# Block 0's triangular steps without GpSimd beside them, block 1's steps moved beside block 0's dense units, and stores queued behind the next loads

## The chip, the cores and the metric

One core of a Trainium2 chip runs the whole program. Its engines are TensorE (PE in the profile; its weight loads are PEld), VectorE (DVE), ScalarE (ACT), GpSimd (POOL) and SyncE (SP), whose queue issues the DMAs. The metric is device time in microseconds (us), the median of repeated runs. Beside these stands one profiled execution, from which every duration below comes.

## The reference, cut to what matters

Three stages follow one another: a delta-rule attention over 4 batches, 8 heads, 768 steps of width 48; a gated feed-forward layer on the 3072 tokens (384 to 2048 to 384); and a dense mixture of 8 experts (384 to 1024 to 384) weighted by a balanced gate.

```python
k_n = k / (np.linalg.norm(k, axis=-1, keepdims=True) + 1e-06)
...
    y[:, :, t] = np.einsum('bhd,bhde->bhe', q[:, :, t], state)
    v_old = np.einsum('bhde,bhd->bhe', state, kt)
    state = state + bt[:, :, :, None] * np.einsum('bhd,bhe->bhde', kt, vt - v_old)
...
h = x @ w_in
sp = np.where(h > 20.0, h, np.log1p(np.exp(np.minimum(h, 20.0))))
g = h * np.tanh(sp)
return (g @ w_out).astype(np.float32)
...
    h = np.maximum(x @ w1[e], 0.0)
    ye = h @ w2[e]
    out += P[:, e:e + 1] * ye
```

## The kernel before

**Blocks and units.** The sequence is cut into 6 blocks of 128 steps for each batch and head. The recurrence of a block becomes a unit triangular system, solved in closed form, and only the state (48 by 48 per batch and head) passes from block to block. After a block's attention, its 512 tokens go through dense units: 16 units of the feed-forward layer (`s0` to `s15`) and 8 units of expert 0 (`s16` to `s23`); `MARKS` counts these places, with four more, `f1` to `f4`, between the two layers. Experts 1 to 7 follow after all blocks. In one dense unit TensorE runs nine matmuls of 512 columns into `psh` (L299) and nine more (L840), each product in three passes of a high and a low part: `xh`, `xl`, `gh` and `gl` are such parts.

**Attention of a block.** Scores of the keys (`st_g`, L590 and L591) land in `gx`; `mb` (`prep_mb`, L539) is the mask with the norms, put on block 0's scores as they leave PSUM (L570) and on block 1's afterwards by GpSimd (`mask_g`, L612). `lane_in_ops` brings the 32 by 32 diagonal blocks into the tile `lane` by transposes, one of all partitions (L622) and two of 32 partitions (L623), and `elim_ops` inverts them in 60 dependent steps on `lane`, a product (L635) and a sum (L641) in turn. `st_lane_out` transposes back (L650, L651). Then TensorE works through `st_m1` (L677), `st_m2` (L691) and the chain of stages z, w, s, y for both pairs (L711, L729, L747, L763) up to `x1` (L770), from which ScalarE makes `xh` (L773) and VectorE `xl` (L458, a helper's line that many VectorE operations share).

**Weights.** The 16 weights of the feed-forward layer arrive as 64-bit numbers. For each, ScalarE scales one half (L205), VectorE decodes in three operations (L188, L191, L196; called a trio below), ScalarE rounds to the high part (L251) and GpSimd subtracts for the low part (L252) into one of six slots `w`. SP stores each converted weight to DRAM (`wd`, L256), and from block 1 on loads it back (L245). Expert weights arrive plain and skip the decoding.

**The prologue.** Block 0's attention runs before any dense unit. `run_warm` puts extra matmuls on the tile `spare` (L874) between its stages. GpSimd meanwhile masks block 0's queries (`mask_p`, L560), scales its values (`prep_v`, L546), and makes and masks block 1's scores. Block 1's 60 steps are dealt out by hand: `elim1` hands most to GpSimd, in the prologue and in the first dense units, and the rest to VectorE, and `drain_elim` or its like closes them at `MARKS[m0]`.

**Order.** Each engine runs its own list in order, waiting on semaphores. Inside the dense units, `fill` and `rate` let queued steps (`eq`) in between by their written costs, and `PLACES` says at which mark each stage of the next blocks stands: for block 0, `m0` is 5 and the steps of block 2 begin at mark 24.

```python
        def elim1(n, eng):
            elim_eng[0] = eng
            for _ in range(min(n, len(ops1))):
                ops1.popleft()()
```

## Time and profile before

| what | us |
|---|---|
| median of 3 runs (2372.46 to 2373.16) | 2372.52 |
| the profiled execution's own time | 2370.98 |
| its span | 2369.2 |
| PE busy | 2298.2 (97%) |
| DVE, ACT, POOL busy | 801.2, 559.9, 471.2 |
| mean granted TensorE clock | 0.971 |

The span is what the instructions cover; the execution's own time lies 1.8 us above it. Busy shares are means over the whole run: TensorE's gaps all lie in the first fifth, where the attention of the blocks is interleaved, so the argument reads that stretch by itself. A record's duration includes time in which an operation stood blocked after it had begun.

### The profile page before, as it was taken

What the parts mean: (1) busy time and instruction counts of PE and PEld (TensorE: products, weight loads), DVE (VectorE), ACT (ScalarE), POOL (GpSimd) and SP (SyncE); (2) the same over time, 40 slices, a digit from 0 to 9 for tenths busy, and PEclk for the clock granted to TensorE, in tenths of its full rate; (3) what the DMA queues carried; (4) which work ended last, traced back from release to release, by engine and by line L of the source; (5) the groups of instructions that cost most, each with busy time, mean ns of one, the idle gap of its engine ahead of it and who ended that gap; (6) DMA issues with size and microseconds to landing.
All of it is one profiled execution on the core that took longest, in us unless ns stands there. A gap on an engine that the chain in (4) does not pass through costs nothing.

```text
span 2369.2 us, 36112 instructions
## 1 busy us (share of the span) xinstructions
PE 2298.2 (97%) x15492; PEld 1992.1 (84%) x15492; DVE 801.2 (34%) x1369; ACT 559.9 (24%) x999; POOL 471.2 (20%) x370
## 2 busy tenths in 40 slices
PE   8688899999999999999999999999999999999998
PEld 4477778878788888899999999999999999999998
DVE  8884725527162104431222222222222122212222
ACT  5244332332323232211211211121121111112111
POOL 5686442341412121310200100020020011001000
PEclk6799999999999999999999999999999999999999
DMA  5357643637344454410100100010010001000111
GB/s 173 134 195 211 211 154 129 211 114 238 131 164 148 162 198 140 167 40 1 54 1 1 37 17 1 1 54 1 1 54 1 1 20 34 1 1 27 27 27 27
DMA packets 79727, 196.00 MB, mean 83 GB/s; under 512 B 7696, under 2 KB 50448, under 8 KB 79568
## 3 DMA queue, kind: packets, MB, share of 16 engines
q1 hardware_dynamic: 79568, 193.70, 24.8%
q8 instruction: 122, 2.00, 0.3%
q14 instruction: 37, 0.30, 0.0%
HBM read 161.43 MB, written 32.24 MB: 82 GB/s over the span
## 4 chain that ended last, share of the span: by engine, by line
PE 90%; DVE 6%; DMA 2%; POOL 1%; issue 1%; ACT 0%; SPq 0%; DVEq 0%; POOLq 0%; ACTq 0%
PE psh L299 42%; PE o L321 30%; PE x L840 8%; PE y L321 3%; DVE t L635 1%; DVE lane L641 1%; PE psa L590 1%; PE psa L729 1%; PE psa L763 1%; DVE lane L623 1%; PE psa L711 1%; PE psa L860 1%; PE psa L747 1%; PE psa L677 1%; DMA wd<-w 0%
## 5 line engine op out<-in xcount | busy, mean ns | idle before, releaser
L299 PE MATMUL psh<-xh,w 128*128 128x512 f32 x2052 | 662.7, 404 | 13.7 <-DMA w<-wd 6.7
L314 DVE SCALAR_TENSOR_TENSOR hl<-psh,hh 128x512 fp32r<-128x512 f32 x384 | 265.1, 690 | 1111.8 <-ACT hh L313 1111.7
L313 ACT ACTIVATE hh<-psh 128x512 fp32r<-128x512 f32 x384 | 229.7, 598 | 1312.1 <-PE o L321 1154.5
L299 PEld LDWEIGHTS psh<-xh,w 128*128 128x128 f32 x2052 | 381.1, 191 | 91.2 <-issue 12.2
L299 PE MATMUL psh<-xl,w 128*128 128x512 f32 x1026 | 412.0, 402 | 4.2 <-DVE xl L458 4.2
L321 PE MATMUL o<-w,hh 128*128 128x384 f32 x1584 | 405.5, 337 | 0.0
L321 PEld LDWEIGHTS o<-w,hh 128*128 128x128 f32 x1584 | 288.2, 188 | 19.8 <-issue 4.9
L321 PE MATMUL o<-wx,hh 128*128 128x384 f32 x1104 | 282.0, 336 | 0.0
L321 PE MATMUL o<-w,hl 128*128 128x384 f32 x792 | 267.0, 337 | 0.0
L299 PE MATMUL psh<-xh,wx 128*128 128x512 f32 x828 | 258.3, 393 | 0.0
L299 PEld LDWEIGHTS psh<-xl,w 128*128 128x128 f32 x1026 | 196.3, 191 | 51.2 <-DVE xl L458 5.9
L321 PEld LDWEIGHTS o<-wx,hh 128*128 128x128 f32 x1104 | 201.5, 188 | 13.1 <-issue 2.1
L829 POOL TENSOR_TENSOR gl<-x,gh 128x512 fp32r<-128x512 f32 x96 | 127.5, 1328 | 420.0 <-ACT gh L828 416.2
L252 POOL TENSOR_TENSOR w<-raw,w 128x768 fp32r<-128x768 f32 x41 | 75.7, 1848 | 669.9 <-ACT w L251 669.8
L321 PE MATMUL o<-wx,hl 128*128 128x384 f32 x552 | 186.0, 337 | 0.0
L299 PEld LDWEIGHTS psh<-xh,wx 128*128 128x128 f32 x828 | 153.5, 188 | 25.2
L299 PE MATMUL psh<-xl,wx 128*128 128x512 f32 x414 | 163.4, 395 | 0.0
L840 PE MATMUL x<-gh,w 128*128 128x512 f32 x576 | 150.7, 397 | 0.0
L321 PEld LDWEIGHTS o<-w,hl 128*128 128x128 f32 x792 | 148.6, 188 | 0.0
L840 PEld LDWEIGHTS x<-gh,w 128*128 128x128 f32 x576 | 107.5, 189 | 24.9
L252 POOL TENSOR_TENSOR wx<-raw,wx 128x768 fp32r<-128x768 f32 x23 | 42.4, 1845 | 399.7 <-ACT wx L251 399.7
L321 PEld LDWEIGHTS o<-wx,hl 128*128 128x128 f32 x552 | 103.6, 188 | 0.0
(165 smaller groups left out, 2358.2 us busy)
## 6 DMA issues: line engine op xcount, KB each, us to landing
w<-wd SPq DMA_DIRECT2D x120, 768.0 KB, 4.4
raw<-in_w_dram SPq DMA_DIRECT2D x128, 192.0 KB, 2.6
wd<-w SPq DMA_DIRECT2D x24, 768.0 KB, 4.3
kq<-in_qkb_dram SPq DMA_DIRECT2D x20, 256.0 KB, 6.9
vt<-in_vtok_dram SPq DMA_DIRECT2D x6, 768.0 KB, 8.6
kq<-in_w_in_dram SPq DMA_DIRECT2D x12, 384.0 KB, 4.7
kq<-in_w_out_dram SPq DMA_DIRECT2D x12, 384.0 KB, 5.6
y0d<-xr SPq DMA_DIRECT2D x6, 768.0 KB, 4.7
```

The source lines that it names most:

```text
L252: nc.gpsimd.tensor_tensor(out=w[:, 1], in0=r, in1=w[:, 0].bitcast(F32), op=ALU.subtract)
L299: mm(ps, lhsT=wi(u, pw, kc), rhs=(xh, xl)[px][:, kc, :], start=(n == 0), stop=(n == 3 * KD - 1))
L313: nc.scalar.activation(out=h, in_=ps, func=AF.Relu)
L314: nc.vector.scalar_tensor_tensor(out=l, in0=ps, scalar=0.0, in1=h.bitcast(F32), op0=ALU.max, op1=ALU.subtract)
L321: mm(o[t], lhsT=(h, l)[ph][:, t * 128:(t + 1) * 128], rhs=wo(u, pw, 0, DM), start=(f == 0 and n == 0), stop=(f == U2 - 1 and n == 2))
L590: mm(ps[0:64, :, i], lhsT=k[64:64 + D, 0, h, :], rhs=k[64:64 + D, 0:2, h, :], start=True, stop=True)
L623: + [(1.14, lambda p=p: nc.vector.transpose(out=lane[p:p + 32], in_=v[p:p + 32, 32:64, :])) for p in (32, 96)]
L635: eng[0].tensor_tensor(out=slot[0], in0=lane[:, s + 1:32, s:s + 1].to_broadcast([128, n, s]), in1=lane[:, s:s + 1, 0:s].to_broadcast([128, ...
L641: eng[0].tensor_tensor(out=lane[:, s + 1:32, 0:s], in0=lane[:, s + 1:32, 0:s], in1=slot[0], op=ALU.add)
L677: mm(ps[p + 32:p + 64, i], lhsT=g[p:p + 32, t, h, 32:64], rhs=t11[p:p + 32, b, :], start=True, stop=True)
L829: nc.gpsimd.tensor_tensor(out=l, in0=p, in1=h.bitcast(F32), op=ALU.subtract)
L840: mm(x2ps[c][k], lhsT=wo(u, pw, k * 128, k * 128 + 128), rhs=(h, l)[pg], start=(f == 0 and n == 0), stop=(f == U1 - 1 and n == 2))
```

## The change

Seven edits, with the names used below.

1. Block 0's steps get VectorE to themselves: `mask_p(0)`, block 1's `mb` and `mask_g(1)` leave the stretch of the steps, and `prep_v(0)` goes from GpSimd to ScalarE (`prep_v_act`). Block 1's squares (`prep_ss(1)`) and norms come later, the norms by a GpSimd power (`prep_pow`) instead of ScalarE's root and VectorE's `root_ops`.
2. One transpose into `lane` instead of three (`lane_in_one`), after ScalarE has copied the diagonal blocks of two partition groups into place (`diag_left`); GpSimd clears the copies afterwards (`diag_clear`). `lane_in_ops` stays for blocks 2 to 5.
3. All 60 steps of block 1 go to VectorE, through the queue `eq`, beside block 0's dense units, closed at mark 9 (`m0` 9 instead of 5); the chain of block 1 and the scores of block 2 move to later marks, block 2's steps to mark 26 (24 before). `rate` is 0.6 in block 0 (0.4 before).
4. The prologue decodes and converts 4 weights (6 decoded, 5 converted before).
5. A weight's store goes to SP after the next raw loads (`late_stores`).
6. The stores of `y0` and `x2` go later in their block (`late_xr`).
7. `load_vt(0)` stands before `load_kq(1)`.

```diff
+    late_stores = deque()
+
+    def flush_stores():
+
+        while late_stores:
+            late_stores.popleft()()
...
-        if ch in w_dram:
-            nc.sync.dma_start(out=w_dram[ch], in_=w.bitcast(F32))
         n = order_of[i] + 2
         if n < len(firsts):
             if kind(firsts[n]) == "plain":
                 fetch(firsts[n])
+        flush_stores()
+        if ch in w_dram:
+            late_stores.append(lambda: nc.sync.dma_start(out=w_dram[ch], in_=w.bitcast(F32)))
...
+        def diag_left(c, t):
+
+            g = gx(c)[:, t]
+            for p in (32, 96):
+                nc.scalar.activation(out=g[p:p + 32, :, 0:32], in_=g[p:p + 32, :, 32:64], func=AF.Copy)
+
+        def diag_clear(c):
+            for p in (32, 96):
+                nc.gpsimd.memset(gx(c)[p:p + 32, :, :, 0:32].rearrange("p t h x -> p (t h) x"), 0.0)
+
+        def lane_in_one(c):
+            v = gx(c).rearrange("p t h x -> p x (t h)")
+            return [
+                (1.94, lambda: nc.vector.transpose(out=lane, in_=v[:, 0:32, :])),
+                (0.09, lambda: nc.vector.memset(lane.rearrange("p t i -> p (t i)")[:, 0:1024:33], 1.0)),
+                (0.0, lambda: diag_clear(c)),
+            ]
...
-            nc.sync.dma_start(out=y0_dram[c], in_=y)
+            late_xr.append(lambda: nc.sync.dma_start(out=y0_dram[c], in_=y))
...
-            for _, op in lane_in_ops(0):
+                diag_left(0, t)
+            for _, op in lane_in_one(0):
                 op()
...
-            for t in range(4):
-                prep_ss(1, t)
-            prep_root(1)
...
-            el(12)
-            for op in root_ops(1) + norm_ops(1, ALL):
-                el(1)
-                op()
             for t in range(4):
-                prep_mb(1, t, nc.gpsimd)
+                prep_ss(1, t)
             for t in range(2):
-                mask_p(0, t)
-            for t in range(2):
-                prep_v(0, t)
                 first_r(0, t)
-            for t in range(4):
-                mask_g(1, t, nc.gpsimd)
-            for t in range(2, 4):
-                prep_v(0, t)
-                mask_p(0, t)
-            for n in range(3):
+            for n in range(2):
                 begin_decode(n)
-            el(len(e0) - 16)
+            el(len(e0) - 24)
...
-            in1 = deque(op for _, op in lane_in_ops(1))
-            in1.popleft()()
-            elim_eng = [nc.gpsimd]
-            ops1 = deque(op for _, op in elim_ops(1, elim_eng))
...
+            prep_pow(1, ALL)
+            for op in norm_ops(1, ALL):
+                op()
+            for t in range(2):
+                mask_p(0, t)
+            for t in range(2):
+                prep_mb(1, t, nc.gpsimd)
...
-            step(4, 6, 5, 6)
             converts(4)
+            for t in range(2, 4):
+                prep_mb(1, t, nc.gpsimd)
+            for t in range(4):
+                mask_g(1, t, nc.gpsimd)
+                diag_left(1, t)
+            eq.extend(lane_in_one(1) + elim_ops(1))
...
-            (5, spread(5 + 3, 26, 2, 16), 21 - 5,
-             [21 - 2, 21 - 1, 21, 21 + 1], spread(21, 27, 2, 8), 18, 26, 24),
+            (9, [12, 12, 13, 13, 14, 14, 15, 15, 17, 18, 19, 19, 20, 20, 21, 21], 16,
+             [19, 20, 22, 23], [22, 22, 23, 23, 24, 24, 25, 26], 18, 26, 26),
...
-                rest[MARKS[m0]].append(drain_elim if c else lambda: elim1(60, nc.vector))
+                rest[MARKS[m0]].append(drain_elim)
...
-                rate(0.4 if c == 0 else 0.6)
+                rate(0.6)
...
-                    if not c and f < m0:
-                        elim1(10, nc.gpsimd)
```

The built programs differ most at four places. On VectorE at the end of the prologue, before, the three operations for `xl` stand behind a group of block 1's steps:

```order
L635 TENSOR_TENSOR t_160<-lane 128x220 [waits Pool_49]
L641 TENSOR_TENSOR lane<-lane,t_160 128x11x20 [waits DVE_49]
L635 TENSOR_TENSOR t_160<-lane 128x210 [waits DVE_49]
L641 TENSOR_TENSOR lane<-lane,t_160 128x10x21 [waits DVE_49]
L635 TENSOR_TENSOR t_160<-lane 128x198 [waits DVE_49]
L641 TENSOR_TENSOR lane<-lane,t_160 128x9x22 [waits DVE_49]
L458 TENSOR_TENSOR xl_1199<-psa,xh_1198 128x512 [waits Activation_49] x3
L458 TENSOR_TENSOR us_155<-psa,us_156 48x384 [waits PE_49]
```

Now, on VectorE at the same place (line numbers are those of the changed file: L655 is the transpose into `lane`, L467 the helper), the last trio of the prologue and block 1's transpose stand ahead of them:

```order
L188 TENSOR_SCALAR bits_168<-bits_168 128x768 [waits DMAHW7_49,DMAHW6_49]
L191 SCALAR_TENSOR_TENSOR bits_168<-bits_168 128x768 [waits DVE_49,Activation_49]
L196 SCALAR_TENSOR_TENSOR bits_168<-bits_168 128x768 [waits DVE_49]
L655 STREAM_TRANSPOSE lane<-gx_146 128x1024 [waits Activation_49,Pool_49]
L467 TENSOR_TENSOR xl_1177<-psa,xh_1176 128x512 [waits DVE_49,Activation_49]
L467 TENSOR_TENSOR xl_1177<-psa,xh_1176 128x512 [waits Activation_49] x2
L656 MEMSET lane 128x32 [waits DVE_49]
```

What moved: VectorE reaches `xl` after a transpose that waits for ScalarE and GpSimd, where before it waited for ScalarE and a GpSimd step. On GpSimd at the same place, before, conversions alternate with steps on `lane`:

```order
L252 TENSOR_TENSOR w_87<-bits_167,w_87 128x768 [waits DMAHW5_49,DMAHW4_49,Activation_49]
L635 TENSOR_TENSOR t_160<-lane 128x234 [waits Pool_49]
L641 TENSOR_TENSOR lane<-lane,t_160 128x13x18 [waits Pool_49]
L635 TENSOR_TENSOR t_160<-lane 128x228 [waits Pool_49]
L641 TENSOR_TENSOR lane<-lane,t_160 128x12x19 [waits Pool_49]
L252 TENSOR_TENSOR w_88<-bits_168,w_88 128x768 [waits DMAHW7_49,DMAHW6_49,Activation_49]
```

Now, on GpSimd, the same conversions and then block 1's masks (L548 makes two `mb`, L627 is `mask_g`), ahead of the first dense unit's `gl` (L867):

```order
L260 TENSOR_TENSOR w_87<-bits_167,w_87 128x768 [waits DMAHW5_49,DMAHW4_49,Activation_49]
L260 TENSOR_TENSOR w_88<-bits_168,w_88 128x768 [waits DMAHW7_49,DMAHW6_49,Activation_49]
L548 TENSOR_TENSOR p_173<-mask_sb,bn_154 128x512
L548 TENSOR_TENSOR p_174<-mask_sb,bn_154 128x512
L627 TENSOR_TENSOR gx_146<-gx_146,s_171 128x512
L627 TENSOR_TENSOR gx_146<-gx_146,s_172 128x512
L627 TENSOR_TENSOR gx_146<-gx_146,p_173 128x512 [waits Pool_49]
L627 TENSOR_TENSOR gx_146<-gx_146,p_174 128x512 [waits Pool_49]
L867 TENSOR_TENSOR gl<-x_175,gh 128x512 [waits Activation_49]
L650 MEMSET gx_146 32x32x32 [waits DVE_49,Pool_49]
```

What moved: the steps left GpSimd, and six masks came in behind the fourth conversion. On ScalarE at this place, now, the copies of `diag_left` (L646) stand ahead of `xh` (L806); before, `xh` followed the conversions directly:

```order
L259 ACTIVATE w_88<-bits_168 128x768 [waits DVE_49]
L646 ACTIVATE gx_146<-gx_146 32x8x32 [waits Pool_49]
L646 ACTIVATE gx_146<-gx_146 32x8x32
L646 ACTIVATE gx_146<-gx_146 32x8x32 [waits Pool_49]
L646 ACTIVATE gx_146<-gx_146 32x8x32
L646 ACTIVATE gx_146<-gx_146 32x8x32 [waits Pool_49]
L646 ACTIVATE gx_146<-gx_146 32x8x32
L646 ACTIVATE gx_146<-gx_146 32x8x32 [waits Pool_49]
L646 ACTIVATE gx_146<-gx_146 32x8x32
L806 ACTIVATE xh_1176<-psa 128x512 [waits PE_49,Activation_49]
```

What moved: eight copies, four of which wait for GpSimd's masks, came ahead of `xh`. On VectorE in block 0's dense units, now, five steps stand between two trios; before there was no step between the trios there:

```order
L188 TENSOR_SCALAR kq_134<-kq_134 128x768 [waits DMAHW6_49,DMAHW5_49]
L191 SCALAR_TENSOR_TENSOR kq_134<-kq_134 128x768 [waits DVE_49,Activation_49]
L196 SCALAR_TENSOR_TENSOR kq_134<-kq_134 128x768 [waits DVE_49]
L668 TENSOR_TENSOR t_160<-lane 128x220
L674 TENSOR_TENSOR lane<-lane,t_160 128x20x11 [waits DVE_49]
L668 TENSOR_TENSOR t_160<-lane 128x228 [waits DVE_49]
L674 TENSOR_TENSOR lane<-lane,t_160 128x19x12 [waits DVE_49]
L668 TENSOR_TENSOR t_160<-lane 128x234 [waits DVE_49]
L188 TENSOR_SCALAR kq_135<-kq_135 128x768 [waits DMAHW2_49,DMAHW1_49]
L191 SCALAR_TENSOR_TENSOR kq_135<-kq_135 128x768 [waits DVE_49,Activation_49]
```

What moved: block 1's 60 steps now run through eight trios up to the transposes out of `lane`. On SP at the start of block 1, before, `y0`'s store and block 2's key loads stand ahead of the fifth reload:

```order
L245 DMA w_88<-wd_93 128x1536 [waits DMAHW7_49,PE_49]
L810 DMA y0d_73<-xr 128x1536 [waits DMAHW0_49,DVE_49,Activation_49]
L468 DMA kq_137<-in_qka_dram 48x1024 [waits DMAHW1_49]
L469 DMA kq_137<-in_qkb_dram 64x2x512 [waits DMAHW2_49]
L468 DMA kq_138<-in_qka_dram 48x1024 [waits DMAHW3_49]
```

Now, on SP, the store stands three reloads after those key loads:

```order
L478 DMA kq_140<-in_qkb_dram 64x2x512 [waits DMAHW7_49]
L253 DMA w_89<-wd_94 128x1536 [waits DMAHW0_49,PE_49]
L253 DMA w_1178<-wd_95 128x1536 [waits DMAHW1_49,PE_49]
L253 DMA w_85<-wd_96 128x1536 [waits DMAHW2_49,PE_49]
L848 DMA y0d_73<-xr 128x1536 [waits DMAHW3_49,DVE_49,Activation_49]
```

What moved: the key loads and three reloads no longer stand behind the store, which waits for VectorE and ScalarE.

## Rows read from the trace of the kernel before

**Rows 1.** TensorE's waits, first 320 us: waiter, releaser, total, times, longest.
```profile
PE psa L763 <- DVE us L458: 6.7, 1, 6.7
PE psh L299 <- DMA w<-wd: 6.7, 1, 6.7
PE psa L729 <- DVE r L458: 5.5, 2, 4.1
PE psa L590 <- issue: 5.5, 1, 5.5
```

**Rows 2.** TensorE's timeline at landmarks: start, duration, engine, line, [idle before it].
```profile
53.76 5.28 PE L874 MATMUL spare<-f 128*128 128x512 f16 x12 [7.57 <-DVE f L963]
61.71 0.38 PE L677 MATMUL psa<-t,gx 32*32 32x32 f32 x13 [2.68 <-DVE t L650]
...
105.14 1.47 PE L770 MATMUL psa<-id_sb,yd 128*128 128x128 f32 x12
...
115.11 0.79 PE L299 MATMUL psh<-xl,w 128*128 128x512 f32 x1 [4.18 <-DVE xl L458]
...
144.90 2.21 PE L677 MATMUL psa<-t,gx 32*32 32x32 f32 x128
...
233.90 2.74 PE L860 MATMUL psa<-wg_sb,xr 128*128 128x8 f32 x24
...
302.06 0.31 PE L677 MATMUL psa<-t,gx 32*32 32x32 f32 x8
```

**Rows 3.** Windows: stretch, length, busy by engine (instructions), granted clock, DMA share, GB/s.
```profile
28.20:54.90 26.70, 19.13 (x127) 12.27 (x124) 25.88 (x26) 11.49 (x30) 24.13 (x20) 0.50 0.37 132
115.00:176.00 61.00, 54.64 (x633) 44.01 (x635) 49.61 (x43) 29.34 (x43) 53.11 (x44) 0.89 0.58 201
224.00:234.00 10.00, 8.22 (x43) 6.71 (x43) 2.37 (x7) 2.35 (x5) 8.64 (x8) 0.51 0.99 224
```

**Rows 4.** VectorE's timeline, prologue: block 0's two small transposes.
```profile
17.08 3.86 DVE L623 STREAM_TRANSPOSE lane<-gx 32x1024 f32<-32x1024 f32 x2
```

**Rows 5.** VectorE's groups, 395 to 434 us (block 3's steps): busy, mean ns | idle.
```profile
L641 DVE TENSOR_TENSOR lane<-lane,t 128x30 f32<-128x30 f32 (+14 forms) x30 | 9.9, 332 | 1.0
L635 DVE TENSOR_TENSOR t<-lane 128x30 f32<-128x30 f32 (+14 forms) x30 | 9.9, 331 | 0.9
```

**Rows 6.** VectorE's groups, 115 to 176 us.
```profile
L191 DVE SCALAR_TENSOR_TENSOR kq<-kq 128x768 int32<-128x768 int32 x7 | 12.7, 1808 | 3.4 <-ACT kq L205 2.8
L196 DVE SCALAR_TENSOR_TENSOR kq<-kq 128x768 int32<-128x768 int32 x6 | 11.5, 1913 | 0.2
...
L458 DVE TENSOR_TENSOR xl<-psa,xh 128x512 fp32r<-128x512 f32 x3 | 1.9, 685 | 0.0
```

**Rows 7.** VectorE's timeline: first two operations of a trio while GpSimd rests.
```profile
163.19 0.56 DVE L188 TENSOR_SCALAR kq<-kq 128x768 int32<-128x768 int32 x1
163.86 0.96 DVE L191 SCALAR_TENSOR_TENSOR kq<-kq 128x768 int32<-128x768 int32 x1
```

**Rows 8.** GpSimd's groups, whole run, from the page: busy, mean ns | idle.
```profile
L829 POOL TENSOR_TENSOR gl<-x,gh 128x512 fp32r<-128x512 f32 x96 | 127.5, 1328 | 420.0 <-ACT gh L828 416.2
L252 POOL TENSOR_TENSOR w<-raw,w 128x768 fp32r<-128x768 f32 x41 | 75.7, 1848 | 669.9 <-ACT w L251 669.8
```

**Rows 9.** GpSimd's groups, 28 to 176 us.
```profile
L612 POOL TENSOR_TENSOR gx<-gx,p 128x512 f32<-128x512 f32 x2 | 2.7, 1350 | 1.9 <-ACT gx L555 1.9
...
L539 POOL TENSOR_TENSOR p<-mask_sb,bn 128x512 f32<-128x512 f32 x2 | 2.3, 1189 | 0.0
```

**Rows 10.** VectorE's timeline, block 0's last units: first and last of block 2's steps.
```profile
254.79 2.06 DVE L622 STREAM_TRANSPOSE lane<-gx 128x1024 f32<-128x1024 f32 x1
...
290.89 2.04 DVE L650 STREAM_TRANSPOSE t<-lane 128x1024 f32<-128x1024 f32 x1
```

**Rows 11.** The chain of waits, pieces in order of time: start, us, what (one dense unit).
```profile
127.65 2.11 PE psh L299 x9
129.77 2.08 PE x L840 x9
```

More of the change, by code (lines that the diff above doesn't have):

```diff
@@ L551, in prep_v, with prep_v_act @@
             prep_scale(c, t, vt(c), nrms[c % 2][1])
+        def prep_v_act(c, t):
+            ne = nrms[c % 2][1]
+            for h in range(H):
+                x = vt(c)[:, t, h * D:h * D + D]
+                nc.scalar.activation(out=x, in_=x, func=AF.Copy, scale=ne[:, t * H + h:t * H + h + 1])
         def raw(out, in_):
@@ L794, in delta_mish_sinkhorn_kernel, with flush_xr @@
         y0ps = {}
+        late_xr = deque()
+        def flush_xr():
+            while late_xr:
+                late_xr.popleft()()
         def y0_second(u):
@@ L853, in x2_done @@
             if c < NBLK - 1:
-                nc.sync.dma_start(out=x2_dram[c], in_=xr)
+                late_xr.append(lambda: nc.sync.dma_start(out=x2_dram[c], in_=xr))
         def logits(c):
@@ L966, in delta_mish_sinkhorn_kernel, with work @@
             st_lane_out(0)
-            in1 = deque(op for _, op in lane_in_ops(1))
-            in1.popleft()()
-            elim_eng = [nc.gpsimd]
-            ops1 = deque(op for _, op in elim_ops(1, elim_eng))
-            def elim1(n, eng):
-                elim_eng[0] = eng
-                for _ in range(min(n, len(ops1))):
-                    ops1.popleft()()
+            prep_pow(1, ALL)
[5 more added lines that the diff above has]
+                prep_mb(1, t, nc.gpsimd)
+            def work(decode, make):
+                decodes(decode)
+                converts(make)
             run_warm(2048, lambda: st_m1(0, 0), lambda: st_m1(0, 1))
             st_place(0, 0, (0, 2))
-            while in1:
-                in1.popleft()()
             run_warm(2048, lambda: st_m2(0, 0))
-            def step(pool, decode, make, dve):
-                elim1(pool, nc.gpsimd)
-                decodes(decode)
-                elim1(dve, nc.vector)
-                converts(make)
-            step(8, 1, 0, 0)
+            work(1, 1)
             run_warm(1536, lambda: st_w(0, 0), lambda: st_w(0, 1))
@@ L992, in delta_mish_sinkhorn_kernel @@
             run_warm(1280, lambda: st_m2(0, 1))
-            step(8, 2, 1, 0)
+            for t in range(2, 4):
+                mask_p(0, t)
+            begins(3)
+            work(2, 1)
             run_warm(1024, lambda: st_s(0, 0), lambda: st_s(0, 1))
@@ L997, in delta_mish_sinkhorn_kernel @@
                 fetch(n)
-            begin_decode(3)
-            step(4, 3, 2, 0)
+            work(2, 2)
             run_warm(1024, lambda: st_z(0, 2), lambda: st_z(0, 3))
-            step(4, 4, 2, 8)
+            begins(4)
+            work(3, 2)
             run_warm(512, lambda: st_w(0, 2), lambda: st_w(0, 3))
-            begins(6)
-            step(2, 5, 3, 0)
+            work(4, 3)
             run_warm(512, lambda: st_y(0, 2), lambda: st_y(0, 3))
@@ L1007, in delta_mish_sinkhorn_kernel @@
                 fetch(n)
-            step(4, 6, 5, 6)
             converts(4)
+            for t in range(2, 4):
+                prep_mb(1, t, nc.gpsimd)
+            for t in range(4):
+                mask_g(1, t, nc.gpsimd)
+                diag_left(1, t)
+            eq.extend(lane_in_one(1) + elim_ops(1))
             early_ctx.close()
@@ L1121, in delta_mish_sinkhorn_kernel @@
                         y0_done(c - 1)
+                    if f == 4:
+                        flush_xr()
                     if f == 2 or not c:
```

11 lines of the change are left out of this document (8 added, 3 removed).

## The prediction

> **What bounds the kernel now.** I read TensorE's waits first [rows 1], then its timeline [rows 2], then VectorE and GpSimd by window [rows 3]. TensorE does nearly all the work, so the change can only move its gaps. In the first 320 us these are a wait of 7.57 in the prologue, for VectorE to come to the end of block 0's steps; 2.68 for the transpose behind them; 6.7 for `us` ahead of stage y; 4.18 for `xl` at the first dense unit; 5.5 for `r` in stage w; 5.5 put down to issue ahead of block 2's scores; and 6.7 for a reloaded weight in block 1 [rows 1, 2]. What the reader is to see next is that VectorE and GpSimd obstruct each other. In 28.2 to 54.9, VectorE ran 26 operations, 24 of them steps, in 25.88 us while GpSimd was busy for 24.13 [rows 3]: 1.0 each, where block 3's 60 steps average 0.33 [rows 5]. In 115 to 176 both are nearly full, and a decode operation that takes 0.96 alone [rows 7] averages 1.81 and 1.91 [rows 6]. Twenty-six operations in 25.88 us against twenty of GpSimd in 24.13: while GpSimd works, VectorE gets through about one operation per GpSimd operation, whatever its own length.
>
> **The prologue (edits 1, 2, 4, 7).** Without GpSimd, the 24 steps return 25.9 less 24 times 0.4 (the large steps, above the mean of 0.33), some 16 us of VectorE; the two transposes return 3.86 [rows 4]. Not all of that is on the path: TensorE's own score work ends at 53.76 - 7.57 = 46.19 [rows 2], so its waits of 7.57 and 2.68 are what goes, 10.2, and stage m1 comes at about 51.5 instead of 61.71. The copies of `diag_left(0)`, the values scaled on ScalarE and the squares moved behind the scores lie under those 46 us; if that cover failed they would cost a few us of the ten. The norms of block 1 now stand on VectorE ahead of the copies behind m1 and wait for GpSimd's power; VectorE has slack there, and I put it at 0, at most some 5 us if the power is late. Between m1 and `x1` TensorE waited 6.7 for `us` behind stretched steps and trios; the steps are gone, two trios of six are too, and I credit 4. So `x1` comes at 105.1 - 10.2 - 4 = 91.
>
> **A new wait at the first dense unit.** The order shows a chain: the fourth trio, its conversion on GpSimd, two masks, four more masks, eight copies on ScalarE, and only then `xh`; and on VectorE the transpose ahead of `xl`. Its price: conversion 1.85 [rows 8], two masks at 1.19 and four at 1.35 [rows 9], 7.8, plus copies, `xh`, the transpose and `xl` (1.9 for three, [rows 6]), some 5 together; from a trio that ends at about 89, the full unit starts at 101 to 104. Before it started at 115.11 [rows 2]. Edit by edit the prologue offers 14 and this chain takes some of it back: TensorE is ahead by about 11 to 12, with 8 to 14 as bounds.
>
> **Block 0's units (edit 3), the largest term.** Before, GpSimd made most of block 1's steps; now VectorE has all of them, and they must end before block 1's m1. From the transpose at about 101, its list has 60 steps of 0.33, 19.9 [rows 5]; eight trios of 0.56 + 0.96 and a third operation like the second, 2.48, so 19.8 [rows 7]; three transposes of 2.06, 6.2 [rows 10]; `xl` 1.9 [rows 6] and four `us`, smaller, by an estimate from it 2; and about 100 gaps of some 0.04, 4. That is 53.8, so 155 if nothing obstructs. TensorE by itself would be at mark 9 at about 103 plus nine units of 4.2 and 2.6 for a stage, near 144 [rows 11]: VectorE is the bound even so. GpSimd in that time has nine `gl` of 1.33, eight conversions of 1.85 [rows 8] and about eight smaller masks and scalings of 0.8 to 1, about 25 operations and 34 us. By one VectorE operation per GpSimd operation, each of 25 holds VectorE for 1.35 where its own (60 steps and 24 decode operations) averages 0.47: 25 times 0.88 = 22. So m1 of block 1 comes at 155 + 22 = 177. From there to the logits, before took 233.90 - 144.90 = 89.0 [rows 2]. Take off the waits in it, 4.1 + 5.5 [rows 1], and four units that now run ahead of m1, 16.8; leave about 3 for the waits behind `r` that remain. That gives 65.6, and logits at 242.6 instead of 233.9: 8.7 late. Ends: with no obstruction 155, logits at 220.6, 13 early; with all 34 us added, 189, logits at 254.6, 21 late. I take 22 because the same steps and the same decode operations show it in [rows 3, 6], both with GpSimd nearly full; here it is busy for under half, and each of its operations still stands in front of VectorE's next.
>
> **Block 1 (edits 5, 6 and the marks).** The wait of 6.7 for a reload goes: the reloads no longer queue behind `y0`'s store. Delayed stores elsewhere I put at 0: their data is read a block later. But block 2's steps start two marks later, about 8.6. VectorE needed 290.89 + 2 + 2 - 254.79 = 40 from its first transpose to the last [rows 10]; from 254.79 + 8.7 + 8.6 this ends at 312. TensorE without the reload wait would be there at 302.06 - 6.7 + 8.7 = 304. So one wait is traded for another, and m1 of block 2 comes at 312 to 313 instead of 302.06, about 10.5 late. From there blocks 2 to 5 and the experts run as before and I know of no slack that would take it back. The sum is 2370.98 + 10.5 = 2381.5 against the profiled execution; the median lies 1.5 above that execution, so 2383.
>
> **Two rules of the Trainium skill.** In [rows 3] the 25.88 and 24.13 us of a 26.7 us window add to 50, so records of both engines overlap. The Trainium skill (SBUF — State Buffer, Who interferes with whom) says that VectorE and GpSimd share a port pair, and that an operation with two SBUF inputs, or in a two-port mode, is held for the whole of a GpSimd operation that reads SBUF; taken as an exclusive lock it gives the end above with all 34 us added. The trace agrees that VectorE is held; that the hold is mutual and complete no row shows. In [rows 3] the granted clock was 0.51, the 1.2 GHz level, in 224 to 234, behind the wait of 5.5. The Trainium skill (TensorE: Matmul & The Clock Gate, Part 1) says that the reduced clock is the default and activity releases it; by that, gaps in each unit could cost more than themselves, and the trace agrees for that one gap.
>
> **The rivals.**
> *VectorE fits (faster).* If GpSimd's operations fall where VectorE idles or reads PSUM, the hold is small: m1 at 155 to 160, logits 8 to 13 early, about the same at block 2, since its steps shift with the units. Time 2360 to 2366. For it: GpSimd is busy less than half of the stretch. Against it: 53.8 us of list already exceeds TensorE's 41, so VectorE never idles there. It decides below about 13 us of hold. Chance 0.22.
> *They cancel.* A hold near 12 to 16 us gives the prologue back and no more: 2369 to 2377. Chance 0.17. That edit 1 does nothing is not a case I give a chance: between its first masks and `mask_p` GpSimd's list holds only two clears and the power.
> *Full exclusion.* Both engines' times add, 34 us of hold: logits 21 late, 2393 to 2395. For it: the stretched decode operations of [rows 6]; against it, overlapping records. Chance 0.10.
> *The clock falls in the paced units.* TensorE would be busy some 4.2 in each 7.7; if it fell to 0.51 as in [rows 3], nine units of up to 8.4 instead of 7.7 add 6: 2388 to 2390. Chance 0.09. It decides only if the gaps are single and long, as that one was; they may be split.
>
> **How the numbers follow.** My forecast, a hold of 17 to 28 us, has the remaining 0.42. A change under 0.2%, 4.7 us, cannot be told from none here. Slower has 0.42 + 0.10 + 0.09 = 0.61, same 0.17, faster 0.22. The likeliest time is 2383, its own range 2377 to 2389; the range for 8 in 10 leaves out the far end of the fast case and that of full exclusion: 2362 to 2393.
>
> **What would show it.** Right: block 0's steps near 0.33 with GpSimd empty; m1 near 51; `xh` waiting for `diag_left`, with the first full unit at 101 to 104; units 1 to 9 longer than TensorE's work, with waits for `w` behind trios of 4 or more us; m1 of block 1 near 177, logits near 243; no wait for the reload but one for block 2's transposes, near 8. Wrong: steps beside the units near 0.4, m1 of block 1 before 165, or a wait at mark 9 that later stages take back.

## The result and the profile after

The changed kernel takes 2385.72 us (median of 4 runs, 2381.68 to 2388.89) where the kernel before, timed between them on the same chip, takes 2372.49. The ratio is 1.0057 (95% interval 1.0042 to 1.0072): slower by about 13 us, with 2383 forecast. The profiled execution is the fastest of the four, 2381.68, with a span of 2379.9 against 2369.2, so its trace shows 10.7 of the 13 us.

The page: busy time, share of the span and instructions of each engine.

```profile
PE 2292.4 (96%) x15492; PEld 1987.4 (84%) x15492; DVE 801.0 (34%) x1407; ACT 573.3 (24%) x1046; POOL 438.6 (18%) x325
```

TensorE is busy for 6 us less than before and the span is 10.7 longer, so by these sums the loss is idle time; what the granted clock adds to it is told below. TensorE's waits in the first 330 us, as in [rows 1] (waiter, releaser, total, times, longest):

```profile
PE psa L710 <- DVE t L683: 24.2, 3, 10.8
PE psh L308 <- ACT x L860: 15.1, 7, 3.2
PE psh L308 <- issue: 10.5, 1, 10.5
PE psa L762 <- DVE gx L695: 5.5, 2, 4.7
PE psa L762 <- DVE r L467: 2.8, 2, 2.2
```

The reload wait of [rows 1] and the long wait for `us` are gone. In their place stand three waits for the transpose behind a block's steps (L683: 5.3, 10.8 and 8.0), seven in block 0's dense units, one of 10.5 ahead of the first of them, and 5.5 for `gx` in the prologue.

TensorE's timeline at the landmarks of [rows 2], in order: m1 of block 0, the transposes of `x1`, the first dense unit and its first `xl`, m1 of block 1, the logits, m1 of block 2.

```profile
41.95 1.28 PE L710 MATMUL psa<-t,gx 32*32 32x32 f32 x40 [5.34 <-DVE t L683]
...
83.54 1.47 PE L803 MATMUL psa<-id_sb,yd 128*128 128x128 f32 x12
...
95.93 1.19 PE L308 MATMUL psh<-xh,w 128*128 128x512 f32 x2 [10.49 <-issue]
98.06 0.80 PE L308 MATMUL psh<-xl,w 128*128 128x512 f32 x1 [0.93 <-DVE xl L467]
...
175.41 1.29 PE L710 MATMUL psa<-t,gx 32*32 32x32 f32 x41 [10.80 <-DVE t L683]
...
237.65 1.51 PE L898 MATMUL psa<-wg_sb,xr 128*128 128x8 f32 x13
...
307.15 3.62 PE L710 MATMUL psa<-t,gx 32*32 32x32 f32 x128 [8.04 <-DVE t L683]
```

Against [rows 2] TensorE is 19.8 ahead at the first m1, 17.1 at the first `xl`, then 30.5 late at m1 of block 1 (which edit 3 puts four units later in TensorE's list), 3.8 late at the logits, 5.1 late at m1 of block 2. Further landmarks (before, after) are the logits of block 1, 394.4 and 402.0; m1 of block 3, 434.2 and 441.9; the logits of block 2, 533.9 and 544.9; m1 of block 5, 717.1 and 727.8. The last 10.7 late stay so to the end.

The windows that answer to the first two of [rows 3], and then one dense unit by itself:

```profile
28.20:54.90 26.70, 19.48 (x289) 11.65 (x285) 18.09 (x39) 22.96 (x105) 9.17 (x4) 0.71 0.41 144
115.00:176.00 61.00, 35.50 (x140) 24.75 (x142) 58.45 (x65) 20.28 (x30) 32.40 (x23) 0.83 0.61 206
123.50:131.00 7.50, 4.71 (x19) 3.31 (x19) 6.85 (x9) 2.79 (x4) 3.19 (x2) 1.00 0.64 212
```

Between 115 and 176, VectorE is busy for 58.45 of 61 us and TensorE for 35.50: a dense unit takes 7.5 us, VectorE fills it, and TensorE stands by in each. This is how it looks inside one, VectorE first and GpSimd below:

```profile
120.88 0.39 DVE L674 TENSOR_TENSOR lane<-lane,t 128x220 f32<-128x220 f32 x1
121.30 0.40 DVE L668 TENSOR_TENSOR t<-lane 128x228 f32<-128x228 f32 x1
121.73 1.93 DVE L674 TENSOR_TENSOR lane<-lane,t 128x228 f32<-128x228 f32 x1
123.69 1.38 DVE L668 TENSOR_TENSOR t<-lane 128x234 f32<-128x234 f32 x1
```

```profile
121.55 1.86 POOL L260 TENSOR_TENSOR w<-kq,w 128x768 fp32r<-128x768 f32 x1 [3.49 <-ACT w L259]
123.53 1.29 POOL L867 TENSOR_TENSOR gl<-x,gh 128x512 fp32r<-128x512 f32 x1
```

Two steps of some 0.40 run freely. The third starts behind GpSimd's conversion and ends just after it, at 1.93; the fourth does the same with `gl`, at 1.38. Each GpSimd operation holds one step, for about its own length. ScalarE's conversion waits for the trio, and behind it in ScalarE's queue stands the activation that empties `psh` (L860): that is how VectorE's load appears as TensorE waiting for `x`.

### The profile page after: what moved, and what is told of

The parts are those of the page before. It is cut to its first block, busy times and chain, and to the rows that moved or that the text cites. A ratio compares the mean times of both kernels' runs of the same rounds, so it can differ in the third digit from the quotient of the medians.

```text
span 2379.9 us, 36164 instructions
## 1 busy us (share of the span) xinstructions
PE 2292.4 (96%) x15492; PEld 1987.4 (84%) x15492; DVE 801.0 (34%) x1407; ACT 573.3 (24%) x1046; POOL 438.6 (18%) x325
## 4 chain that ended last, share of the span: by engine, by line
PE 89%; DVE 7%; DMA 1%; issue 1%; ACT 1%; POOL 1%; SPq 0%; DVEq 0%; ACTq 0%; POOLq 0%
PE psh L308 41%; PE o L330 30%; PE x L878 8%; PE y L330 3%; DVE t L668 1%; DVE lane L674 1%; PE psa L762 1%; PE psa L605 1%; PE psa L796 1%; PE psa L744 1%; PE psa L898 1%; DMA kq<-in_qka_dram 1%; PE psa L724 1%; PE psa L710 1%; PE psa L780 1%
## 5 line engine op out<-in xcount | busy, mean ns | idle before, releaser
L330 PEld LDWEIGHTS o<-w,hh 128*128 128x128 f32 x1584 | 288.1, 188 | 19.9 <-issue 5.0
L867 POOL TENSOR_TENSOR gl<-x,gh 128x512 fp32r<-128x512 f32 x96 | 124.6, 1298 | 417.5 <-ACT gh L866 409.6
L878 PE MATMUL x<-gh,w 128*128 128x512 f32 x576 | 156.3, 408 | 0.4 <-issue 0.4
```

The source lines that it names most:

```text
L330: mm(o[t], lhsT=(h, l)[ph][:, t * 128:(t + 1) * 128], rhs=wo(u, pw, 0, DM), start=(f == 0 and n == 0), stop=(f == U2 - 1 and n == 2))
L867: nc.gpsimd.tensor_tensor(out=l, in0=p, in1=h.bitcast(F32), op=ALU.subtract)
L878: mm(x2ps[c][k], lhsT=wo(u, pw, k * 128, k * 128 + 128), rhs=(h, l)[pg], start=(f == 0 and n == 0), stop=(f == U1 - 1 and n == 2))
```

## The experiments

Ratios are against the kernel before, timed side by side with each kernel, with 95% intervals. Landmarks come from the profile of each.

**The stores alone.** The kernel before with edits 5 and 6:

```diff
-        if ch in w_dram:
-            nc.sync.dma_start(out=w_dram[ch], in_=w.bitcast(F32))
...
+        flush_stores()
+        if ch in w_dram:
+            late_stores.append(lambda: nc.sync.dma_start(out=w_dram[ch], in_=w.bitcast(F32)))
...
-            nc.sync.dma_start(out=y0_dram[c], in_=y)
+            late_xr.append(lambda: nc.sync.dma_start(out=y0_dram[c], in_=y))
...
```

> The kernel before with the delayed stores alone (edits 5 and 6). Theory: the wait of 6.7 us for a reloaded weight in block 1 goes; block 2's transposes end near 295 us, so m1 of block 2 can come at 295 to 297 instead of 302.06, and the total falls by 5 to 7 us, to about 2366. Rival, that another wait takes its place as it did in the changed kernel (8.04 us for the transpose): block 2's steps start where they did, so within 2 us of 2372.5.

Measured: 2366.29, ratio 0.9970 (0.9958 to 0.9981), m1 of block 2 at 290.2. The reload wait is gone and the stores alone make the kernel before faster, by 7.6 us at the medians of the runs timed side by side, as expected. Put on top of the stores, the rest of the change then costs some 20 us.

The lead at m1 of block 2 is 11.9, more than expected. Of this 3.2 were there ahead of the reload, from a stretch that no run takes apart; 6.7 is the wait, and 1.8 is what the nine matmuls behind it took longer in the kernel before. Half of the lead is lost again, first inside m1, by a wait that the profile puts to no engine:

```profile
PE psa L686 <- issue: 3.5, 1, 3.5
```

The work behind it starts at the low clock (0.88 from 290.2 to 318), and stage m2 starts only 6.1 earlier than before. So the rival, another wait in the old one's place, is half right.

This profile showed something else. Its prologue is that of before, yet the granted clock is not: windows of before, then of this kernel.

```profile
18.00:34.00 16.00, 16.00 (x156) 10.84 (x157) 15.29 (x37) 12.57 (x52) 5.83 (x5) 0.50 1.05 307
```

```profile
18.00:34.00 16.00, 14.36 (x206) 9.81 (x204) 15.26 (x38) 15.59 (x58) 6.17 (x6) 1.00 1.04 310
```

With the clock at 1.2 GHz TensorE was busy for all 16 us over 156 matmuls; at 2.4 GHz it got through 206. Still m1 of block 0 came at 61.3 here and at 61.7 before, because VectorE ended the stretch; TensorE just waits longer:

```profile
PE spare L888 <- DVE f L977: 21.9, 1, 21.9
```

So the 7.57 of [rows 2] was what the low clock had left of a wait of 21.9.

**The chain ahead of the first unit.** The changed kernel with block 1's last two `mb`, `mask_g`, `diag_left` and the transpose behind `xh` and `xl`:

```diff
-            for t in range(2, 4):
-                prep_mb(1, t, nc.gpsimd)
-            for t in range(4):
-                mask_g(1, t, nc.gpsimd)
-                diag_left(1, t)
-            eq.extend(lane_in_one(1) + elim_ops(1))
             early_ctx.close()
...
             run(*[lambda kc=kc: st_x1(0, kc) for kc in range(KD)])
+            for t in range(2, 4):
+                prep_mb(1, t, nc.gpsimd)
+            for t in range(4):
+                mask_g(1, t, nc.gpsimd)
+                diag_left(1, t)
+            eq.extend(lane_in_one(1) + elim_ops(1))
```

> The changed kernel with block 1's masks, the eight copies and the transpose into lane placed behind xh and xl instead of ahead of them. Theory (VectorE's list sets m1 of block 1): the first full dense unit comes about 10 us earlier, near 88, but VectorE's list ends no earlier, so m1 of block 1 stays at 173 to 179, TensorE's waits move into the paced units, and the total stays within 3 us of 2385. Rival (the wait of 10.5 us at the first unit is itself the loss): everything from the first unit on comes 10 us earlier, 2375.

Measured: 2378.47, ratio 1.0029 (1.0014 to 1.0043). The first unit starts at 88.9 instead of 95.9, so the chain was what held it; m1 of block 1 comes at 170.2, 5.2 earlier, the logits and m1 of block 2 each 3.3 earlier. The spans differ by only 1.9, the ratios by some 6.6 us, and these runs do not settle which is nearer. The result lies between the two expectations. VectorE's transpose starts at 96.1 instead of 95.3, so its list does not begin sooner; but `xl` (2.1) now runs while VectorE waits for the transpose, and the 2.9 that it waited for `us` behind it are gone. That is how part of the 7 us passes through; a third of it is lost again by the logits.

**The steps.** The changed kernel without block 1's 60 steps, which it leaves out:

```diff
-            eq.extend(lane_in_one(1) + elim_ops(1))
+            eq.extend(lane_in_one(1))
```

> The changed kernel without block 1's 60 steps (block 1's triangular inverse is left out, so block 1's attention is wrong; all else runs). Theory: the steps cost VectorE 20 us of their own and most of the hold; the units run at TensorE's pace, 4.2 to 5 us each, m1 of block 1 comes near 140 to 148 instead of 175.4, the logits 25 to 33 us earlier, and the total falls by 25 to 33, to 2352 to 2360. Rival (the decode trios and conversions alone pace the units): m1 at 160 or later, total 2370 or more.

Measured: 2357.66, ratio 0.9938 (0.9919 to 0.9957); m1 of block 1 at 148.7 instead of 175.4. Waits from 80 to 180 us of this kernel, then of the changed one:

```profile
PE psa L710 <- DVE t L683: 2.8, 1, 2.8
...
PE psh L308 <- ACT x L860: 1.5, 2, 0.8
```

```profile
PE psh L308 <- ACT x L860: 15.1, 7, 3.2
PE psa L710 <- DVE t L683: 10.8, 1, 10.8
```

Without the steps both waits nearly go. The steps cost 26.7 us at m1 of block 1 and 28 of the median: in this stretch VectorE is the bound, and nothing later gives it back.

**GpSimd's hold.** The changed kernel in which block 0's first nine units leave `gl` out and read `gh` in its place:

```diff
             nc.scalar.activation(out=h, in_=p, func=AF.Copy)
+            if u < 9:
+                gh[u], gl[u] = h, h
+                return
```

> The changed kernel without GpSimd's nine operations for gl in block 0's first nine units (TensorE reads gh in their place, so the low part of these products is left out). Theory (one VectorE operation is held per GpSimd operation): nine holds of about 0.9 us go, m1 of block 1 comes 6 to 10 us earlier, near 167, and the total falls by as much. With full exclusion nine times 1.3, 12 us. Rival (VectorE's own list is the length, holds cost little): within 2 us of 175.4 and of 2385.

Measured: 2376.13, ratio 1.0016 (0.9998 to 1.0034); m1 of block 1 at 167.9, 7.5 earlier, and the waits for `x` fall to

```profile
PE psh L308 <- ACT x L860: 8.5, 6, 1.7
```

Without nine operations of GpSimd m1 comes 7.5 us earlier, 0.83 each; counted from block 1's transpose, which starts 0.7 later in this profile, it is 8.2. A full lock would have given nine times 1.3, 11.7, and no hold would have given nothing. That it is a hold of VectorE's own operations, and no wait between them, shows in its records from that transpose to m1 of block 1, of the changed kernel and of this one: the same steps and trios take 9.0 us less, 8.5 of it in these lines.

```profile
L668 DVE TENSOR_TENSOR t<-lane 128x30 f32<-128x30 f32 (+14 forms) x30 | 21.8, 728 | 0.9
L674 DVE TENSOR_TENSOR lane<-lane,t 128x30 f32<-128x30 f32 (+14 forms) x30 | 20.7, 691 | 0.8
...
L188 DVE TENSOR_SCALAR kq<-kq 128x768 int32<-128x768 int32 x8 | 7.9, 984 | 0.0
```

```profile
L674 DVE TENSOR_TENSOR lane<-lane,t 128x30 f32<-128x30 f32 (+14 forms) x30 | 20.3, 676 | 0.8
L668 DVE TENSOR_TENSOR t<-lane 128x30 f32<-128x30 f32 (+14 forms) x30 | 17.2, 573 | 0.9
...
L188 DVE TENSOR_SCALAR kq<-kq 128x768 int32<-128x768 int32 x8 | 4.4, 551 | 0.0
```

**The norms out of the way.** The changed kernel with block 1's norms and first two `mb` behind the copies of m1:

```diff
             prep_pow(1, ALL)
-            for op in norm_ops(1, ALL):
-                op()
...
             work(1, 1)
+            for op in norm_ops(1, ALL):
+                op()
...
```

> The changed kernel with block 1's norms on VectorE, and the first two masks made from them, placed behind the first decode trio instead of ahead of the copies that follow block 0's m1. Theory: VectorE's wait of 7.42 us for GpSimd's power goes, the copies start near 44 us instead of 54.96, and all that follows on VectorE's list comes 7 to 10 us earlier: the first dense unit near 87 instead of 95.9, m1 of block 1 near 167, the total near 2377. Rival (the power, late on GpSimd, holds the masks and so the first dense unit anyway): the first unit stays at 94 to 96 and the total at 2383 or more.

Measured: 2385.72, ratio 1.0065 (1.0049 to 1.0081): nothing gained. VectorE's copies behind m1, in the changed kernel and here:

```profile
51.02 1.23 DVE L538 TENSOR_SCALAR ne<-ne 128x32 f32<-128x32 f32 x1 [7.42 <-POOL ne L516]
...
54.96 1.39 DVE L467 COPY mb<-psa 32x512 f32<-32x512 f32 x2
```

```profile
55.23 1.39 DVE L467 COPY mb<-psa 32x512 f32<-32x512 f32 x2 [11.84 <-PE psa L710]
```

The wait of 7.42 for the power is gone and the copies stand 3.3 behind the start of m1 (51.9 in this profile) instead of 13.0. Yet from m1 of block 0 to m1 of block 1 it takes 131.2 where it took 133.5. The rival holds: VectorE's wait lay for the most part beside the path. That the chain by which block 1's transpose comes late runs through GpSimd, from the power over the masks and conversions, is read from the order of its list; this run does not show it.

This profile also has the low clock that before had, and here it is not hidden: m1 of block 0 starts at 51.9, 10 later than in the changed kernel's profile. Window of this kernel and of the changed one:

```profile
18.00:30.00 12.00, 12.00 (x130) 7.86 (x126) 10.90 (x33) 6.26 (x15) 1.55 (x2) 0.50 1.03 240
```

```profile
18.00:30.00 12.00, 10.74 (x157) 7.24 (x157) 10.90 (x33) 11.63 (x41) 1.80 (x2) 1.00 1.06 256
```

**Block 1's steps earlier.** The same with all masks and copies behind the norms, and the transpose and first steps ahead of stage y:

```diff
...
             work(4, 3)
+            eq.extend(lane_in_one(1) + elim_ops(1))
+            fill(8.0)
             run_warm(512, lambda: st_y(0, 2), lambda: st_y(0, 3))
...
-                mask_g(1, t, nc.gpsimd)
-                diag_left(1, t)
-            eq.extend(lane_in_one(1) + elim_ops(1))
```

> As the run with the later norms, and block 1's masks and copies stand on GpSimd and ScalarE right behind those norms, its transpose and some 8 us of its steps on VectorE behind the fourth decode trio, ahead of xh and xl. Theory (VectorE's list from there to block 1's m1 sets the time, so its idle stretches are what can be had back): the wait of 10.5 us at the first dense unit goes, the unit starts at 78 to 84, m1 of block 1 comes at 157 to 164, the total falls by 12 to 18 below the changed kernel, to 2367 to 2374. Rival (GpSimd's masks, now ahead of block 0's second masks and conversions, hold block 0's own chain): x1 and the first unit later than with the later norms alone.

Measured: 2370.03, ratio 0.9998 (0.9988 to 1.0009); m1 of block 1 at 162.6, 12.8 earlier, though m1 of block 0 comes 3.6 later in this profile. The first unit starts at 93.8, not at the 78 to 84 expected: `xh` and `xl` still queue behind the work that was put ahead of them (waits of 4.8 and 2.8). The transpose starts at 87.1 instead of 95.3, so that 8.2 of the 12.8 come from the list's early start; the unit itself starts only 2.2 earlier.

**Block 2's m1 two marks later.** On top of it:

```diff
-            (3, spread(3 + 3, 19, 1, 16), 8 - 5,
+            (5, spread(5 + 3, 21, 1, 16), 8 - 5,
```

In this kernel block 3's masks take the place of two tiles that block 2's m2 still reads, so that m2 is computed from other data.

> As the run with the early transpose, and in block 1's dense units m1 of block 2 and its chain stand two marks later (5 instead of 3). Theory (the wait of 8.04 us for block 2's transpose exists because its steps begin two marks later while its m1 stayed): most of that wait goes, m1 of block 2 has no or under 2 us of wait, and the logits of block 1 come 4 to 8 us earlier than in the run without it; total 2360 to 2369. Rival (block 2's chain, two marks later, runs into the end of its block): a new wait at block 2's x1, and no gain in the total.

Measured: 2367.40, ratio 0.9983 (0.9973 to 0.9993). The waits from 190 to 330 us, of the kernel without this edit and with it:

```profile
PE psa L710 <- DVE t L683: 8.0, 1, 8.0
```

```profile
PE psa L710 <- DVE t L683: 3.3, 1, 3.3
```

TensorE gets two dense units ahead of m1 and most of the wait goes, though 3.3 are left where under 2 were expected.

**The same with block 3's masks and scores moved along** (`[8, 9, 11, 13], spread(10, 21, 1, 8)`), so that m2 reads its own data:

> As the run with the early transpose (e6), and in block 1's dense units m1 of block 2 and its chain stand two marks later, block 3's masks and scores likewise, so that no tile is written before its last reader. Theory (the wait of 8.04 us for block 2's transpose exists because its steps begin two marks later while its m1 stayed): the wait shrinks to 0 to 4 us, the logits of block 1 come 4 to 8 us earlier counted from block 0's logits, total 3 to 8 us below e6, near 2365. Rival (the wait moves to a later stage): same as e6, 2370.

Measured: 2367.87, ratio 0.9991 (0.9979 to 1.0004), the same wait of 3.3. From the logits of block 0 to those of block 1 it takes 160.2 where the kernel without the move took 164.0, so the profile shows 3.8; the medians show 2.2, which these intervals cannot separate.

**Norms early by ScalarE's root.** On top of that:

```diff
-            prep_pow(1, ALL)
+            for op in root_ops(1) + norm_ops(1, ALL):
+                op()
+            prep_mb(1, 0, nc.gpsimd)
```

with block 1's squares and root ahead of the score copies on ScalarE, and its values scaled there instead of on VectorE.

> As e8, with block 1's squares on ScalarE ahead of the scores' copies, its norms by ScalarE's root and VectorE behind block 0's transposes (no power on GpSimd), block 0's values scaled behind the scores, block 1's values scaled on ScalarE. Theory (GpSimd's list from the norms on, begun only at 51 us by the power, holds block 0's chain in the prologue): GpSimd's masks start near 45, the first dense unit comes 5 to 9 us earlier than in e8 counted from block 0's m1, the four holds of GpSimd's scalings go from the units (3 us), total 5 to 12 us below e8, 2353 to 2360. Rival (block 0's chain is held by the raw weights or by TensorE's own stages): first unit and total as in e8.

Measured: 2363.12, ratio 0.9961 (0.9946 to 0.9975), 4.8 below the step before by the medians and 7 by the ratios, where 5 to 12 were expected, but not in the expected way. Counted from m1 of block 0, block 1's transpose starts at 41.5 where it was 43.6 in the step before, and the first unit at 48.1 where it was 50.3: 2.1 earlier and not 5 to 9 (m1 of block 0 itself comes 4.0 later in this profile). So the theory that GpSimd's list from the norms on holds block 0's chain does not come out; `xh` and `xl` are waited for again (2.2 and 3.3). It is the fastest of the kernels that leave nothing out, faster than both kernels, though its interval and that of the stores alone overlap.

**Which store was it, and what is lost behind block 2?** Two kernels from the changed one, with edit 5 alone undone and with edit 6 alone undone.

```diff
+        if ch in w_dram:
+            nc.sync.dma_start(out=w_dram[ch], in_=w.bitcast(F32))
...
-        flush_stores()
-        if ch in w_dram:
-            late_stores.append(lambda: nc.sync.dma_start(out=w_dram[ch], in_=w.bitcast(F32)))
```

> The changed kernel with edit 5 alone undone: a converted weight's store is issued at once, ahead of the next plain loads, as in the kernel before; the stores of y0 and x2 stay late. Theory: what the delayed stores gain, 7.6 us in the kernel before, came from edit 6 (the reloads at the start of block 1 no longer stand behind y0's store), so here no wait of some 6 us for a reload of w comes back, and block 1 starts m1 of block 2 within 1.5 of 307. The stretch from m1 of block 3 to the logits of block 2 stays near 103. Total within 3 us of the changed kernel's median of 2385.7. Rival: the conversions' stores were what the reloads stood behind; then a wait for w of 4 to 7 us is back at the start of block 1 and the total is 2389 to 2393.

Measured: 2384.08, ratio 1.0050 (1.0033 to 1.0067). No wait for a reload; m1 of block 2 at 308.9, 0.4 beyond the expected bound, with the logits 1.4 late already. The theory holds for the stores of weights in the changed kernel; in the kernel before the two edits were only tried together. It misses in one thing: from m1 of block 3 to the logits of block 2 it takes 99.9, not 103.

```diff
-            late_xr.append(lambda: nc.sync.dma_start(out=y0_dram[c], in_=y))
+            nc.sync.dma_start(out=y0_dram[c], in_=y)
...
-                late_xr.append(lambda: nc.sync.dma_start(out=x2_dram[c], in_=xr))
+                nc.sync.dma_start(out=x2_dram[c], in_=xr)
```

> The changed kernel with edit 6 alone undone: y0 and x2 are stored as soon as they are done; the weights' stores stay behind the next loads. Theory: the wait for a reloaded w, 6.7 us in the kernel before, is back at the start of block 1; as block 2's transpose comes 8.0 late for TensorE anyway, that wait shrinks by as much and m1 of block 2 starts within 2 us of 307, so that in the changed kernel edit 6 earns almost nothing. If edit 6 is also what lengthens the stretch from m1 of block 3 to the logits of block 2 (103.0, in the kernel before 99.7), that falls to 99.5 to 100.5 and the total to 2380 to 2383. Rival: nothing of that stretch belongs to edit 6 (it stays at 103), and the reload wait adds to the rest: m1 of block 2 at 311 to 314, total 2389 to 2393.

Measured: 2386.85, ratio 1.0065 (1.0043 to 1.0088). TensorE's waits from 180 to 350 us, and those of SP's queue from 262 to 310:

```profile
PE psh L308 <- DMA w<-wd: 8.2, 1, 8.2
```

```profile
SPq L848 <- DVE xr L467: 11.2, 1, 11.2
```

SP waits 11.2 for the store's data with the reloads behind it, as it waited 11.1 before; TensorE waits 8.2 for the reload, and not at all for block 2's transpose, so that m1 of block 2 comes at 308.0 against 307.15. In the changed kernel edit 6 trades one wait for another and earns 0.9 us at m1 of block 2, with medians that the intervals cannot separate; in the kernel before, where the transpose was in time, both edits on stores earned 7.6. The stretch of block 3 takes 99.8 here as expected, but the total did not fall, so edit 6 is not shown to cost anything there, and with edit 5 undone it took 99.9 too.

## Why the prediction came out, and where its steps failed

**Prologue, too small by ten.** Forecast m1 of block 0 at 51.5, measured 41.95. The step that failed is "TensorE's own score work ends at 46.19": that work had run at 1.2 GHz in the profile of before, and I did not look at the clock of that window, though the first line of [rows 3] has 0.50. In the changed kernel's profile it ran at 2.4 GHz. With the low clock the term is right, 51.9, as one run above shows by chance. VectorE's side was right: block 0's steps run at 0.19 to 0.41 with GpSimd empty, and the 16 and 3.86 that it was to get back are what it got, its transpose out of `lane` starting at 39.79 instead of 59.55. From m1 to `x1` I credited 4 and got 1.8 (41.6 instead of 43.4). The wait of 6.7 for `us` went, but TensorE now waits 5.5 for `gx`, whose copy (L695) stands on VectorE behind the norms, and these, which I put at 0, wait 7.42 for the power: GpSimd's

```profile
45.55 5.44 POOL L516 TENSOR_TENSOR ne<-ss,half_sb 128x32 f32<-128x32 f32 x1 [25.70 <-ACT sq L510]
```

is longer than the 5 that I had as the bound. With the norms moved TensorE no longer waits for `gx`, yet `x1` comes only 1.1 sooner behind m1, in a profile at the low clock, and the median is no lower.

**The chain ahead of the first unit, right in kind, some 2 too short.** The order mask, `diag_left`, `xh` stands as read, and the first `xl` at 98.06 comes 14.5 behind `x1`'s transposes at 83.54 where 10 to 13 were forecast; the run with the chain put behind confirms it. Its sign in the profile is not `xh` but "issue", a wait that the profile could not name.

**Block 0's units, right in kind, the hold some 5 too small.** From the transpose to m1 of block 1 it takes 175.41 - 95.32 = 80.1 where 76 were forecast. By VectorE's records there, the steps took 42.5 where 19.9 were in the list and the trios 24.6 where 19.8 were: 27.4 of hold beside 27 GpSimd operations of 38.2 us, where 25 operations and 22 were forecast. The hold of 0.88 for each is thus 1.0 over all, and 0.83 by m1 on the nine left out. The sign forecast for it, waits for `w` of 4 or more, did not come: these waits are 1.1 in all, and TensorE waits for `x` instead, up to 3.2.

On the rule of the Trainium skill (SBUF — State Buffer, Who interferes with whom), which calls the port pair an exclusive lock and has the order of issue decide who blocks: VectorE is held as it says, one operation for the length of a GpSimd one (0.40 became 1.93 beside 1.86). In the changed kernel GpSimd's own operations kept the durations of [rows 8], so that the cost is about the GpSimd operation less the VectorE operation that it catches. The kernel without the steps shows the other side. There VectorE has trios, of 0.96 an operation, one behind the other, and GpSimd's operations from the transpose to m1 of block 1 grow too, from 1.87 and 1.31 to

```profile
L260 POOL TENSOR_TENSOR w<-kq,w 128x768 fp32r<-128x768 f32 x8 | 17.0, 2121 | 2.6 <-ACT w L259 2.5
L867 POOL TENSOR_TENSOR gl<-x,gh 128x512 fp32r<-128x512 f32 x9 | 16.6, 1840 | 9.4 <-ACT gh L866 9.0
```

So the hold goes both ways, which [rows 3] alone could not show.

Since the transpose came 5.7 ahead of the forecast's 101, m1 of block 1 came 1.6 ahead of its 177. From there to the logits it takes 62.2 against 65.6, so that the logits came at 237.65, 5 earlier than forecast.

**Block 1, right.** The reload wait went, the wait for block 2's transpose is 8.04 where 8 was forecast, and m1 of block 2 comes 69.5 behind the logits against 69.9. So the trade was read rightly, and the two kernels with m1 two marks later show that it was a matter of the marks.

**"From there as before", wrong by 5.6.** TensorE is 5.1 late at m1 of block 2 and 10.7 late from the logits of block 2 on. A first part is lost straight behind the wait of 8.04, where the granted clock is below that of before: TensorE is 8.8 late at stage m2, of which 1.1 has come back by the logits of block 1 (windows of before, then after):

```profile
302.00:330.00 28.00, 28.00 (x450) 22.68 (x449) 8.91 (x17) 11.50 (x20) 8.96 (x9) 1.00 0.38 125
```

```profile
307.20:335.00 27.80, 27.80 (x433) 22.89 (x434) 10.82 (x21) 10.65 (x18) 12.55 (x7) 0.84 0.31 96
```

The other 3.3 lie behind a stall put to issue in block 3. It is 2.1 here, but the kernel before has one of 1.8 in the same stretch, so the loss is not the stall but the clock behind it (before, after, and the kernel with edit 5 undone):

```profile
434.18:460.00 25.82, 24.01 (x420) 19.63 (x420) 10.46 (x21) 11.03 (x19) 12.66 (x7) 1.00 0.86 257
```

```profile
441.90:467.70 25.80, 23.69 (x403) 19.25 (x404) 9.35 (x19) 10.61 (x18) 10.98 (x6) 0.87 0.55 168
```

```profile
443.30:469.10 25.80, 23.77 (x419) 19.44 (x419) 10.46 (x21) 10.93 (x19) 12.65 (x7) 1.00 0.60 201
```

The third kernel has a stall of 2.0 at the same line of code and keeps 2.4 GHz. Why the clock falls behind one and not behind the other is not settled. The forecast of +10.5 at m1 of block 2 was thus 5.4 too high and the zero behind it 5.6 too low: the total of 2383 came out by luck, by two errors that cancel. Against the profiled execution 2381.5 were forecast and 2381.68 measured. The median came out 2.7 above the forecast, because it lies 4.0 above that execution and not 1.5.

**The rivals.** "VectorE fits" falls: VectorE is idle for under 3 of 61 us there, and the hold is 27 and not below 13. Full exclusion in its stated price, all of GpSimd's time added, falls by the nine `gl` and by 27.4 of 38.2. The clock came and went between the paced units (1.00 from 123.5 to 131, 0.77 in the next one), and fell in the last of them:

```profile
131.00:138.50 7.50, 6.22 (x18) 4.38 (x18) 7.22 (x9) 2.78 (x4) 4.36 (x3) 0.77 0.59 211
...
161.50:170.00 8.50, 3.11 (x8) 1.98 (x8) 8.16 (x11) 2.67 (x4) 5.49 (x4) 0.55 0.57 185
```

That rival had its mechanism but not its price, since VectorE set the pace there: the units behind 123.5 follow one another every 7.1 to 8.1 us, at either clock.

## What to carry to other kernels

When work is moved between two engines, sum the list of the engine that receives it for the stretch in which it must end, and add for each operation of a neighbour that gets in its way about the neighbour's duration less its own (here 27 operations of 38.2 us cost 27.4). Where its own operations are as long as the neighbour's, the neighbour is held too. Before a wait is credited, look at the granted clock of the waiting engine's own work: a low clock can lie hidden under another bound, and so can a high one. Stores that wait for late data belong behind the loads in the same queue, and that is worth something only where the next wait isn't as long.

## What the hardware showed that I had not expected

The first stretch of one and the same program part runs at 1.2 GHz in some executions and at 2.4 GHz in others (0.50 in before and in the run with the norms moved, 1.00 in the changed kernel and in the run of the stores alone, 0.77 to 0.97 in the four kernels with block 1's steps earlier, all from 18 to 30 us). In the kernel with the moved norms the low clock follows a wait of 3.44 for the query loads at 16.48; in before, no wait there is longer than 0.84. It moved m1 of block 0 by 10 us between two kernels where TensorE was the bound there, and by nothing between two where VectorE was. The four runs of the changed kernel are ordered by their mean granted clock (0.974 at 2381.68, then 0.972, and 0.970 at the two longest). That the prologue's clock makes this spread, and puts the median 4 above the profiled run, is an inference that no run here proves.
